# A list scheduler in the kernel in place of a hand-made order: gated linear attention followed by a two-layer MLP

## The chip, the cores and the metric

The kernel runs on one core of a Trainium2 chip. The metric is the device time of one execution in microseconds (us); lower is better. A profiled execution also gives a *span*, from its first to its last instruction.

Ratios are the mean time of one kernel's fast runs over the mean of the other's fast runs of the same rounds, so not quite the ratio of the medians that are quoted beside them. "Fast" leaves out runs that are over 1.5% above the fastest of the same kernel. On both the kernel before spread widely (213.6 to 218.1 us, at granted clocks from 0.984 down to 0.960), so differences between variants are read from their own times and traces, beside a control run of the changed kernel on the first of the two; the changed kernel was not run on the second.

## The reference, cut to what matters

```python
def _attn_ref(q, k, v, alpha):                 # B, H, S, D = 4, 8, 768, 48
    state = np.zeros((B, H, D, D))
    for t in range(S):
        state = alpha[:, :, t, :, None] * state + einsum('bhd,bhe->bhde', k[:, :, t], v[:, :, t])
        y[:, :, t] = einsum('bhd,bhde->bhe', q[:, :, t], state)
    return y

def _moe_ref(x, w_in, w_out):                  # x: 3072 x 384, d_ff = 2048
    return gelu_tanh(x @ w_in) @ w_out         # x: y, the heads side by side
```

The kernel cuts time into six chunks of 128. A chunk of one batch is a unit, two batches of one chunk are a *pair* (twelve pairs), and two pairs are a group.

## The kernel before

For a pair, ScalarE (ACT) takes the logarithm of alpha, PE sums it up over time (`cum`), and ACT takes three exponentials; these are the "decays". VectorE (DVE) multiplies q and k with them. For each unit PE transposes the products, DVE evicts them, PE makes the scores, DVE masks them, PE makes kv and y, and DVE carries the state to the next chunk. y goes through ACT (`x`), is transposed and becomes `xT`, the input of layer 1. Layer 1 needs a gelu on ACT for each of 16 tiles, layer 2 a copy and a store for each result.

The order of all this is written by hand. Ahead of the logarithms the kernel loads the table set that holds ln and exp; the set of the gelu it leaves to the compiler.

```python
LN_EXP_SET = 6
    # ... inside run():
        def decays(p):
            return [lambda: (self.act_set(LN_EXP_SET), self.e_ln(p)),
                    lambda: (self.e_cum(p), self.e_exp(p))]
        # ... the third to sixth pair, for instance:
        run(*decays(p3))
        lc = self.layer1(xT1, gT1, 0, 2)
        _merge(lc, scores(p3), 0.3, 0.9)
        run(*state(p3, xT1, 2)[:2], decays(p4)[0])
        l2 = self.layer2(G[1], gT1, False, 0, 2)
        run(*l2[:1], *state(p3, xT1, 2)[2:], *l2[1:3], decays(p4)[1], *l2[3:])
        # ... groups 3 to 5: layer 1 for a whole group (512 columns), x transposed by DMA
```

The PSUM tiles of layer 1 and layer 2 share one ring of four buffers:

```python
            h = hs[nt] = self.ps.tile([C, (hi - lo) * C], F32, tag="ff", bufs=4, name="hT")
            # ...
            acc[mt] = self.ps.tile([C, self.d_model], F32, tag="ff", bufs=4, name="acc")
```

Of the kernel before, what the change touches and what calls it, by code (L numbers as in the profile page):

```python
# [11 lines left out]
LN_EXP_SET = 6  # L12
DMA_QK = False
# [9 lines left out]
def _merge(main, side, first=0.0, last=1.0):  # L23

    n, m = len(main), len(side)
    lo, hi = first * n, last * n
    at = [lo + (hi - lo) * (i + 0.5) / m for i in range(m)] if m else []
    j = 0
    for i in range(n):
        while j < m and at[j] <= i:  # L30
            side[j]()
            j += 1
        main[i]()
    while j < m:
        side[j]()
        j += 1


class _Kernel:
    def __init__(self, ctx, tc, q, k, v, alpha, w_in, w_out, out):  # L40
# [10 lines left out]
        self.groups = [[(c, b) for b in range(B)] for c in range(self.NCH)]  # L51

        const = ctx.enter_context(tc.tile_pool(name="const", bufs=1))
        self.ld = ctx.enter_context(tc.tile_pool(name="ld", bufs=6))
        self.wk = ctx.enter_context(tc.tile_pool(name="wk", bufs=3))
        self.grp = ctx.enter_context(tc.tile_pool(name="grp", bufs=2))
        self.ps = ctx.enter_context(tc.tile_pool(name="ps", bufs=1, space=bass.MemoryType.PSUM))

        self.ut_h = const.tile([C, C], F16, name="ut_h")
# [4 lines left out]

# [4 lines left out]
        self.NR = 4  # L69
        self.la_ring = [const.tile([C, 2, H, 64], F16, name=f"la{i}") for i in range(self.NR)]  # L70
        self.qp_ring = [const.tile([C, 2, H, 64], BF16, name=f"qp{i}") for i in range(self.NR)]
        self.kp_ring = [const.tile([C, 2, H, 64], BF16, name=f"kp{i}") for i in range(self.NR)]
        self.npair = 0
        self.u = {}
        self.loaded = {}


    def pads(self, ring):
        for t in ring:
            self.nc.vector.memset(t[:, :, :, self.D:64], 0.0)  # L80

    def load(self, n, group, part=None, eng=None):

        C, H, D = self.C, self.H, self.D
        c = group[0][0]
        if (n, c) not in self.loaded:
            self.loaded[n, c] = self.ld.tile([C, len(group), H, D], BF16 if n == "v" else F32, tag=n,
                                             bufs=3, name=n)
        t = self.loaded[n, c]
        lo, hi = (0, len(group)) if part is None else (2 * part, 2 * part + 2)  # L90
        src = self.src[n][lo:hi].rearrange("b h s d -> s (b h) d")[c * C:(c + 1) * C]
        (eng or self.nc.gpsimd).dma_start(t[:, lo:hi].rearrange("t b h d -> t (b h) d"), src)  # L92
        for i in range(lo, hi):
            u = self.u.setdefault(group[i], {})
            u[n] = t[:, i]
            if i % 2 == 0:
                u[n + "pair"] = t[:, i:i + 2]

    def load_w_in(self, part):
        w = self.d_ff // 4  # L100
        sl = slice(part * w, (part + 1) * w)
        self.nc.gpsimd.dma_start(
            self.w_in[:, :, sl], self.w_in_dram.rearrange("(j c) n -> c j n", c=self.C)[:, :, sl])

    def load_w_out(self, part):
        w = self.NFT // 4
        sl = slice(part * w, (part + 1) * w)
        self.nc.gpsimd.dma_start(
            self.w_out[:, sl, :], self.w_out_dram.rearrange("(n c) p -> c n p", c=self.C)[:, sl, :])
# [6 lines left out]


    def e_ln(self, pair):
        u0 = self.u[pair[0]]
        r = u0["ring"] = self.npair % self.NR  # L120
        self.npair += 1
        self.nc.scalar.activation(self.la_ring[r][:, :, :, 0:self.D], u0["apair"], AF.Ln)  # L122

    def e_cum(self, pair):
        nc, D, H = self.nc, self.D, self.H
        u0 = self.u[pair[0]]
        la = self.la_ring[u0["ring"]]
        cum = u0["cum"] = self.ps.tile([self.C, 2, 512], F32, tag="ca", name="cum")
        for i in range(2):
            nc.tensor.matmul(cum[:, i, 0:H * D], self.ut_h, la[:, i, :, 0:D], start=True, stop=True)  # L130
            for p in range(H // 2):
                nc.tensor.matmul(cum[:, i, H * D + p:H * D + p + 1],  # L132
                                 la[:, i, 2 * p:2 * p + 2, :].rearrange("t h d -> t (h d)"),
                                 self.ones, start=True, stop=True, skip_group_check=True)

    def e_exp(self, pair):
        nc, D, H = self.nc, self.D, self.H
        u0 = self.u[pair[0]]
        cum, r = u0["cum"], u0["ring"]
        b8 = self.wk.tile([self.C, 2, H * D], BF16, tag="b8", bufs=2, name="b8")  # L140
        binv8 = self.wk.tile([self.C, 2, H * D], BF16, tag="binv8", bufs=2, name="binv8")
        bend = self.grp.tile([self.C, 2, H // 2], F32, tag="bend", bufs=6, name="bend")
        nc.scalar.activation(b8, cum[:, :, 0:H * D], AF.Exp)  # L143
        nc.scalar.activation(binv8, cum[:, :, 0:H * D], AF.Exp, scale=-1.0)
        nc.scalar.activation(bend, cum[:, :, H * D:H * D + H // 2], AF.Exp)
        qp, kp = self.qp_ring[r], self.kp_ring[r]
        nc.vector.tensor_tensor(qp[:, :, :, 0:D], u0["qpair"],  # L147
                                b8.rearrange("t i (h d) -> t i h d", h=H), op=ALU.mult)
        nc.vector.tensor_tensor(kp[:, :, :, 0:D], u0["kpair"],  # L149
                                binv8.rearrange("t i (h d) -> t i h d", h=H), op=ALU.mult)  # L150
        for i, cb in enumerate(pair):
            self.u.setdefault(cb, {}).update(qp=qp[:, i], kp=kp[:, i], bend=bend[:, i])


    def t_qk(self, cb, evict=None):
        nc, H, C = self.nc, self.H, self.C
        u = self.u[cb]
        t = self.grp.tile([C, 2, H // 2, C], BF16, tag="qkT", bufs=6, name="qkT")
        if DMA_QK:
            nc.sync.dma_start_transpose(t[:, 0], u["qp"].rearrange("t h d -> t (h d)"))  # L160
            nc.sync.dma_start_transpose(t[:, 1], u["kp"].rearrange("t h d -> t (h d)"))
        else:
            ps = self.ps.tile([C, 2, H // 2, C], BF16, tag="yk", bufs=2, name="qkT_ps")
            for j, s in enumerate((u["qp"], u["kp"])):
                for p in range(H // 2):
                    nc.tensor.transpose(  # L166
                        ps[:, j, p, :], s[:, 2 * p:2 * p + 2, :].rearrange("t h d -> t (h d)"), self.ident)
            (evict or nc.vector.tensor_copy)(t, ps)  # L168
        u["qT"], u["kT"] = t[:, 0], t[:, 1]

    def attn(self, cb):
        nc, H, C = self.nc, self.H, self.C
        u = self.u[cb]
        qT, kT = u["qT"], u["kT"]
        at = self.ps.tile([C, 2, H // 2, C], F32, tag="ca", name="at")
        for p in range(H // 2):
            for o in range(2):
                sl = slice(64 * o, 64 * o + 64)
                nc.tensor.matmul(at[:, o, p, :], kT[sl, p, :], qT[sl, p, :], start=True, stop=True)  # L179
        atm = u["atm"] = self.grp.tile([C, 2, H // 2, C], BF16, tag="atm", bufs=6, name="atm")  # L180
        for o in range(2):
            nc.vector.tensor_tensor(atm[:, o], at[:, o],  # L182
                                    self.ut[:, None, :].to_broadcast([C, H // 2, C]), op=ALU.mult)

    def kv(self, cb):
        nc, H, C, D = self.nc, self.H, self.C, self.D
        c, b = cb
        if c == self.NCH - 1:
            return
        u = self.u[cb]  # L190
        kv = self.ps.tile([C, H // 2, 2 * D], F32, tag="yk", bufs=2, name="kv")
        for p in range(H // 2):
            nc.tensor.matmul(kv[:, p, :], u["kp"][:, 2 * p:2 * p + 2, :].rearrange("t h d -> t (h d)"),
                             u["v"][:, 2 * p:2 * p + 2, :].rearrange("t h d -> t (h d)"),
                             start=True, stop=True)
        old, new = self.state[b][c % 2], self.state[b][(c + 1) % 2]
        for o in range(2):
            ps, fs = slice(64 * o, 64 * o + 64), slice(D * o, D * o + D)
            acc = kv[ps, :, fs]
            if c > 0:  # L200
                s = self.wk.tile([C, H // 2, D], F32, tag=f"stmp{o}", name="stmp")
                nc.vector.tensor_tensor(s[ps], acc, old[ps, :, fs], op=ALU.add)  # L202
                acc = s[ps]
# [3 lines left out]
    def y(self, cb, xT, i, dma):  # L207
# [14 lines left out]
        if dma:  # L222
            nc.sync.dma_start_transpose(xT[:, :, i, :], x)
# [10 lines left out]
    def layer1(self, xT, gT, lo=0, hi=4):  # L234
        nc, C = self.nc, self.C
        hs = {}
# [227 lines left out]
```

## Time and profile before

| | before |
|---|---|
| median time | 216.96 us (216.65 to 218.38, 4 runs) |
| span of the profiled run (its time: 214.48) | 212.7 us |
| busy: PE, DVE, ACT, POOL | 86%, 53%, 58%, 25% |
| table loads on ACT | 16 |
| PE matmuls: layer 1, layer 2 | 432, 384 |

The page of a profile gives shares of the whole span; the timeline gives single instructions; the view by windows gives the busy time of each engine in a stretch. Two rows of this last view show weak stretches of the kernel before, after its start. The columns are: from and to, length, then busy time and instructions of PE, of PE's weight loads, DVE, ACT and POOL, granted clock of PE, DMA share and GB/s.

```profile
120.00:132.00 12.00, 9.83 (x110) 6.34 (x107) 9.61 (x22) 6.47 (x12) 0.00 (x0) 0.86 0.27 68
...
175.00:188.00 13.00, 11.92 (x112) 7.54 (x110) 3.49 (x6) 2.14 (x5) 0.00 (x0) 1.00 0.28 77
```

In the first PE is busy for 9.8 of 12 us and runs at a clock of 0.86; its two longest waits there are 1.60 us for a state update by DVE and 0.57 for `x` from ACT. In the second the idle 1.1 us stand at the end, where layer 1 waits for a DMA transpose of `x`. In both the DMA moves 68 to 77 GB/s, beside some 200 earlier, and PE waits for no input.

From 56.6 us on, the waits of PE that the trace of the kernel before names are short and of many kinds: for gelus 2.9 us in all, state updates 2.6, `x` 2.3, a DMA transpose 1.2, a logarithm 0.8, an eviction 0.5.

### The profile page before, as it was taken

The numbers are of one execution on the slowest core, as the hardware profiler recorded it, in microseconds if no ns is written. First come the engines' busy times: TensorE is split into PE (matmuls) and PEld (weight loads), VectorE is DVE, ScalarE is ACT, GpSimd is POOL, SyncE is SP. The second block draws the span as 40 slices with busy tenths as digits, with TensorE's granted clock in tenths as the row PEclk, the third lists the DMA queues.
The fourth block names the chain that finished last, engine by engine and source line by source line (L and its number), as shares of the span: only waits on it lengthen the run. The fifth ranks groups of instructions, "written<-read, shape, count | busy, mean of one in ns | idle before, by whom it ended". The sixth has DMA issues, their size and how long they took to land.

```text
span 212.7 us, 4196 instructions
## 1 busy us (share of the span) xinstructions
PE 183.7 (86%) x1734; PEld 118.1 (56%) x1740; DVE 111.9 (53%) x224; ACT 124.0 (58%) x235; POOL 53.9 (25%) x51
## 2 busy tenths in 40 slices
PE   7676579997688998998868959999989999979993
PEld 2344468664466586576556645545655546634561
DVE  7372470059658558548578796464895652210121
ACT  3327968641785866586894746758638661149400
POOL 7983753656342344345300000000000000000000
PEclk9999999999799999999999997999999999999999
DMA  7999999999999999999993121100222001310022
GB/s 139 168 222 172 204 207 212 173 171 189 208 248 206 186 183 209 187 192 205 189 168 22 44 70 40 37 3 0 74 77 74 0 3 56 112 57 0 0 74 74
DMA packets 42738, 25.82 MB, mean 121 GB/s; under 512 B 32704, under 2 KB 39360, under 8 KB 42720
## 3 DMA queue, kind: packets, MB, share of 16 engines
q0 software_dynamic: 32208, 19.27, 65.4%
q1 hardware_dynamic: 10512, 6.29, 10.9%
q8 instruction: 13, 0.21, 0.5%
q14 instruction: 5, 0.04, 0.1%
HBM read 25.17 MB, written 4.72 MB: 141 GB/s over the span
## 4 chain that ended last, share of the span: by engine, by line
PE 50%; DMA 20%; POOL 8%; issue 8%; DVE 6%; ACT 6%; SPq 0%; POOLq 0%; ACTq 0%; DVEq 0%
PE acc L270 20%; PE hT L241 19%; DMA w_out<-in_moe_w_out_dram 7%; DMA a<-in_alpha_dram 7%; DMA q<-in_q_dram 5%; PE at L179 3%; PE qkT_ps L166 2%; POOL v L92 2%; DVE atm L182 2%; PE cum L130 2%; POOL q L92 2%; POOL a L92 2%; POOL k L92 2%; DVE qkT L168 2%; DMA xT<-x 1%
## 5 line engine op out<-in xcount | busy, mean ns | idle before, releaser
L241 PE MATMUL hT<-xT,w_in 128*128 128x256 bf16 (+1 forms) x427 | 71.7, 311 | 8.0 <-ACT gT L246 5.6
L246 ACT ACTIVATE gT<-hT 128x256 bf16<-128x256 f32 (+1 forms) x144 | 60.7, 457 | 24.1 <-PE hT L241 22.5
L270 PE MATMUL acc<-w_out,gT 128*128 128x384 bf16 x384 | 68.8, 329 | 0.0
L241 PEld LDWEIGHTS <-w_in 128*128 128x128 bf16 x432 | 40.4, 99 | 27.4 <-issue 9.2
L270 PEld LDWEIGHTS <-gT 128*128 128x128 bf16 x384 | 35.7, 98 | 21.9 <-issue 0.8
L182 DVE TENSOR_TENSOR atm<-at,ut 128x512 bf16<-128x512 f32 x48 | 30.9, 686 | 15.2 <-PE at L179 15.1
L274 DVE COPY ot<-acc 128x384 f32<-128x384 f32 x24 | 13.2, 556 | 33.2 <-PE acc L270 32.8
L221 ACT CAST x<-yps 128x384 bf16<-128x384 f32 x24 | 11.5, 478 | 29.0 <-PE yps L218 26.6
L147 DVE TENSOR_TENSOR qp<-q,b 128x768 bf16<-128x768 f32 x12 | 11.5, 958 | 27.3 <-ACT b L143 27.1
L168 DVE COPY qkT<-qkT_ps 128x1024 bf16<-128x1024 bf16 x21 | 14.5, 691 | 15.1 <-PE qkT_ps L166 15.1
L92 POOL DMA_DIRECT2D v<-in_v_dram x9 | 12.0, 1335 | 16.4 <-issue 9.5
L143 ACT ACTIVATE b<-cum 128x768 bf16<-128x768 f32 x12 | 9.7, 810 | 9.7 <-PE cum L132 9.1
L92 POOL DMA_DIRECT2D q<-in_q_dram x9 | 12.1, 1344 | 11.2 <-issue 7.2
L92 POOL DMA_DIRECT2D k<-in_k_dram x9 | 12.0, 1331 | 7.9 <-DVE stmp L202 3.9
L92 POOL DMA_DIRECT2D a<-in_alpha_dram x8 | 10.8, 1353 | 11.7 <-issue 6.8
L179 PE MATMUL at<-qkT 64*128 64x128 bf16 x192 | 9.5, 218 | 4.7 <-DVE atm L182 3.7
L179 PEld LDWEIGHTS <-qkT 64*128 64x128 bf16 x192 | 5.5, 94 | 11.9 <-DVE qkT L168 6.4
L113 ACT ACT_TABLE_LOAD x9 | 11.5, 1283 | 0.9 <-PEq L448 0.7
L149 DVE TENSOR_TENSOR kp<-k,binv 128x768 bf16<-128x768 f32 x12 | 11.4, 952 | 1.2 <-DMA k<-in_k_dram 1.2
L204 DVE TENSOR_TENSOR st<-stmp,bend 64x192 bf16<-64x192 f32 x32 | 11.3, 353 | 1.4
L122 ACT ACTIVATE la<-a 128x768 f16<-128x768 f32 x12 | 10.0, 842 | 2.9 <-DMA a<-in_alpha_dram 2.8
L202 DVE TENSOR_TENSOR stmp<-kv,st 64x192 f32<-64x192 f32 x32 | 11.3, 353 | 0.5
(41 smaller groups left out, 154.6 us busy)
## 6 DMA issues: line engine op xcount, KB each, us to landing
out_dram<-ot SPq DMA_DIRECT2D x24, 192.0 KB, 2.0
q<-in_q_dram POOLq DMA_DIRECT2D x6, 384.0 KB, 13.1
k<-in_k_dram POOLq DMA_DIRECT2D x6, 384.0 KB, 13.3
a<-in_alpha_dram POOLq DMA_DIRECT2D x3, 768.0 KB, 11.8
q<-in_q_dram POOLq DMA_DIRECT2D x3, 768.0 KB, 11.7
k<-in_k_dram POOLq DMA_DIRECT2D x3, 768.0 KB, 12.4
a<-in_alpha_dram POOLq DMA_DIRECT2D x5, 384.0 KB, 13.1
w_in<-in_moe_w_in_dram POOLq DMA_DIRECT2D x4, 384.0 KB, 9.6
```

What stands on the lines that cost most here:

```text
L92: (eng or self.nc.gpsimd).dma_start(t[:, lo:hi].rearrange("t b h d -> t (b h) d"), src)
L113: nc.scalar.add_instruction(mybir.InstLoadActFuncSet(name=nc.get_next_instruction_name(), act_func_set_id=i, engine=mybir.EngineType.Activ ...
L147: nc.vector.tensor_tensor(qp[:, :, :, 0:D], u0["qpair"], b8.rearrange("t i (h d) -> t i h d", h=H), op=ALU.mult)
L149: nc.vector.tensor_tensor(kp[:, :, :, 0:D], u0["kpair"], binv8.rearrange("t i (h d) -> t i h d", h=H), op=ALU.mult)
L168: (evict or nc.vector.tensor_copy)(t, ps)
L179: nc.tensor.matmul(at[:, o, p, :], kT[sl, p, :], qT[sl, p, :], start=True, stop=True)
L182: nc.vector.tensor_tensor(atm[:, o], at[:, o], self.ut[:, None, :].to_broadcast([C, H // 2, C]), op=ALU.mult)
L221: nc.scalar.copy(x, yps.rearrange("t h d -> t (h d)"))
L241: nc.tensor.matmul(h, self.w_in[:, j, nt * C:(nt + 1) * C], xT[:, j, lo:hi].rearrange("p g t -> p (g t)"), start=j == 0, stop=j == self.NK ...
L246: nc.scalar.activation(gT[:, nt, lo * C:hi * C], hs.pop(nt), AF.Gelu_apprx_tanh)
L270: nc.tensor.matmul(acc[mt], gT[:, nt, mt * C:(mt + 1) * C], self.w_out[:, nt, :], start=nt == 0, stop=nt == self.NFT - 1)
L274: nc.vector.tensor_copy(ot, acc[mt])
```

## The change

The hand-made order is replaced by a list scheduler that runs while the kernel is built. Each task has one engine (or a choice of ACT and DVE), a cost, a priority, its dependences and the buffers that it takes. The recurrence has the highest priority. Layer 1 and layer 2 of all pairs are one stream that keeps its order: layer 1 of pair m, layer 2 of pair m. From the third pair on, the decays of pair m+2 have a fixed slot between the gelus of pair m and those of pair m+1, so that the table sets don't alternate. For the first two pairs, k products and evictions are cut in halves. All x transposes are on PE. The diff, cut to its core:

```diff
-LN_EXP_SET = 6
-DMA_QK = False
+LN_EXP, GELU = 6, 0
+W = dict(
+    ln=760, exp=720, bend=170, gelu4=510, gelu2=340, table=1290,
+    cum=530, t8=450, t4=225, attn=340, kv=170, inter=170, intra=205, tx=168, l1_4=655, l1_2=340, l2=655,
+    # ...
+)
+class Scheduler:
+    # ... of the tasks that can start within 60 ns of the earliest, the one of highest priority:
+                    window = min(f[0] for f in found) + 60
+                    at, t = min((f for f in found if f[0] <= window), key=lambda f: (f[1].prio, f[0]))
+    # ... tasks():
+            early = m < 2
+                    e1 = s.add("ev", {"ACT": W["ev4_act"], "DVE": W["ev4"]}, o, self.turned(u, j, "q"), [t1])
+                g = s.add("gelu", {"ACT": W["gelu2"]}, 10000 + n, self.gelu(f, c, lo, hi, nt),
+                          [t] + free + between[m - 1], GELU)
+                ot = s.add("ot", {"DVE": W["ot"], "ACT": W["ot_act"]}, -1, self.result(f, c, b), [t])
+        for m, ps in decays.items():
+            for p in ps:
+                if m >= 0:
+                    lns[p].deps.append(gs[m][-1])
+    # ... run():
+        for t in order:
+            if t.load is not None:
+                self.act_set(t.load)
+            t.emit(t.engine)
```

## The prediction

> **What bounds the kernel now.** I read the page first (busy shares, slices, chain), then the timelines of PE, ACT and DVE for the first 72 us, those of PE and ACT around 105 us, and the POOL timeline.
>
> ```profile
> PE 183.7 (86%) x1734; PEld 118.1 (56%) x1740; DVE 111.9 (53%) x224; ACT 124.0 (58%) x235; POOL 53.9 (25%) x51
> ...
> PE   7676579997688998998868959999989999979993
> ...
> PE 50%; DMA 20%; POOL 8%; issue 8%; DVE 6%; ACT 6%; SPq 0%; POOLq 0%; ACTq 0%; DVEq 0%
> ```
>
> PE is the busiest engine and half of the chain that ended last. But 86% flatters it: it counts warm-up matmuls on a zero tile and the overlapping tails of pipelined matmuls. So I take the spacing of starts from PE's timeline (start, duration, what):
>
> ```profile
> 32.23 5.40 PE L241 MATMUL hT<-xT,w_in 128*128 128x256 bf16 x48 [0.45 <-DVE xT L231]
> 37.47 4.06 PE L270 MATMUL acc<-w_out,gT 128*128 128x384 bf16 x24
> 41.37 0.33 PE L130 MATMUL cum<-la,ut_h 128*128 128x384 f16 x1
> ```
>
> From 32.23 to 37.47 is 5.24 us for the 16 layer-1 tiles of a pair (three matmuls each, 0.3275 a tile). From 37.47 to 41.37 is 24 layer-2 matmuls, 0.1625 each, so 5.20 for a pair's 32. The same timeline gives, per pair: cum 0.53, transposes of q and k 0.89, scores 0.66, kv 0.35, y 0.75, transposes of x 0.33. Sum **13.95 us per pair**; twelve pairs, less the last kv and the first inter-chunk y, are some 166 us of useful PE work in a span of 212.7. About 46 us are waits, warm-ups and cold clock. Where they begin:
>
> ```profile
> 4.85 0.84 ACT L122 ACTIVATE la<-a 128x768 f16<-128x768 f32 x1 [2.83 <-DMA a<-in_alpha_dram]
> ...
> 9.49 0.96 DVE L149 TENSOR_TENSOR kp<-k,binv 128x768 bf16<-128x768 f32 x1 [1.20 <-DMA k<-in_k_dram]
> ...
> 18.04 0.81 PE L241 MATMUL hT<-xT,w_in 128*128 128x256 bf16 x6 [0.45 <-DVE xT L231]
> ```
>
> Layer 1 starts at 18.0: the first k lands at 9.5 and a serial chain follows, in which PE does only 3.2 us of work. Later, layer 1 repeatedly waits for a gelu that stands behind the next decays and a table load on ACT:
>
> ```profile
> 107.28 0.39 PE L166 MATMUL qkT_ps<-ident,kp 128*128 128x128 bf16 x4
> 109.35 0.82 PE L241 MATMUL hT<-xT,w_in 128*128 128x256 bf16 x6 [1.68 <-ACT gT L246]
> ...
> 107.62 1.28 ACT L246 ACT_TABLE_LOAD   x1
> 108.91 1.67 ACT L246 ACTIVATE gT<-hT 128x256 bf16<-128x256 f32 x5
> ```
>
> The first gelu starts at 108.91 and PE's fifth tile, which needs its PSUM buffer, at 109.35, 0.44 later. I use this pattern below.
>
> **What the Trainium skill says.** "ScalarE: Activation LUTs", What ACT_TABLE_LOAD costs: about 1283 ns for the load plus 1380 ns of drain at each switch. The trace agrees on the load (1283 ns mean, 16 loads) and not on the drain: from 107.62 to the gelu at 108.91 is 1.29. Same page, Table sets: gelu and the tanh approximation of gelu are in separate sets, and a compiler pass puts a load before each activation that needs one. In the trace seven loads carry the gelu's own line, so that pass is at work. "TensorE: Matmul & The Clock Gate", Back-to-back issue gap: 262 cycles for 256 columns, so 109 ns; the 48 above took 109 each, so halving layer 1's tiles costs PE almost nothing. "Perfetto Trace Analysis", Identifying the Most-Contended Engine: matmul busy share is no measure of closeness to the roofline; the 184 busy against 166 of work agrees.
>
> **The change, part by part.** The built order of the changed kernel shows it, engine by engine.
>
> *Work.* Layer 1 goes from 432 to 576 matmuls, all 256 wide; groups 3 to 5 ran 512 wide at 0.215, so this adds 0.6 us. The 12 DMA transposes of x become 36 more PE transposes (2.0 us) and 12 DVE copies. Wide gelus (0.56 apart) become pairs at 0.33 apart: some 5 us on ACT. Warm-up matmuls go from 32 to 39. Loads are the same bytes, all by pair, first ones in the same order.
>
> *A mistake in it.* The scheduler charges one table load per change of set, and the kernel emits it as set 0. The built program puts a second load, of set 11, under the gelu's own line straight after: ten loads of set 0 that no activation uses. ACT has 30 loads in place of 16. Each wasted one is 1.28 us of ACT, 12.8 in all. Does it reach PE?
>
> *Steady period*, pairs 3 to 10, counting from T, the end on PE of the second chunk's y. PE then does x transposes, 28 layer-2 matmuls and cum: 0.165 + 0.65 + 0.165 + 1.95 + 0.53 + 1.95 = 5.41 to the end of layer 2. It goes on with four layer-1 tiles (1.31), transposes (0.89), first scores (0.33) and kv (0.18): 2.7 us, then needs a PSUM buffer that the first new gelu frees. ACT's order between gelus is: load, ln, two exps, bend, copy of the *second* layer-2 result, load, load, gelu. The exps end at T + 0.21 (PE to ACT) + 0.42 (x) + 1.28 + 0.84 + 0.84 (cum and its latency) + 1.55 = T + 5.14. The copy must wait for layer 2's end, T + 5.41 + 0.21 = 5.62, takes 0.45, and two loads end at T + 8.64. Tile 5 starts at T + 9.07. PE got there at T + 8.1, so it **waits 0.95 each period**. With one load the gelu would come 0.3 before it is needed. After tile 5: twelve tiles 3.93, kv 0.18, scores 0.33, two y 0.75, four layer-2 matmuls 0.65, in sum 5.84. Period 5.41 + 3.66 + 5.84 = **14.9** against 13.95 of work. DVE needs about 10 to 11 us a period, ACT 13: neither is the bound alone; it is the loop of both through that copy.
>
> *Start.* Halved k products and halved evictions shorten the chain from k's landing (9.5): products 10.0 and 10.5, evictions on ACT to 11.6, scores, masks, y, x; layer 1 near 16.8, 1.2 earlier. The second pair's inputs do not come earlier. POOL's waits tell their landings:
>
> ```profile
> 16.71 0.74 POOL L108 DMA_DIRECT2D w_out<-in_moe_w_out_dram  x1 [1.35 <-DMA a<-in_alpha_dram]
> 18.82 0.74 POOL L108 DMA_DIRECT2D w_out<-in_moe_w_out_dram  x1 [1.37 <-DMA q<-in_q_dram]
> 20.92 1.17 POOL L92 DMA_DIRECT2D a<-in_alpha_dram  x1 [1.36 <-DMA k<-in_k_dram]
> ```
>
> The new order has ACT do ln (16.7), exps (to 19.9), three evictions, the last waiting for k (to 23), and only then two loads: first gelu near 25.6, where it was 23.0. This takes back the early start. From tile 5 at 26.0, 28 tiles and the rest of the recurrence take 10.3, so both layer-1 halves end at 36.3 (was 37.5). Then two layer-2 pairs (10.4), two cums, and the recurrence of pair 2 with the transposes of pair 3, 16.6 us of PE work with fills, and about 1.3 of waits on x and kp: layer 1 of pair 2 at **54.0**. The old kernel is there at 56.6.
>
> *Sum.* From 54.0: first T at 61.0, the next at 76.4 (its layer 2 falls wholly in the period), then seven periods of 14.9: T of period 10 at 180.7, less 0.2 for missing kv. Then 4.88 of layer 2, 5.24 and 5.20 for the last pair: 195.8. The old kernel's last matmul ended at 209.0 with 3.6 more to the span's end, which I keep: span 199.4. The median time is 1.02 times the span (217.05 to 212.7), so 203.5; I say **204**, as a walk with fixed durations misses small waits.
>
> **The rivals.**
> *The second load is hidden.* If the copy does not wait, or the period has slack that I missed, PE is the bound at 13.95: 7.6 us less, about 196. For it: the order was made from durations near the trace's. Against: with the load counted, 3.76 us on ACT stand against 2.7 on PE.
> *The fixed order slips.* One wrong duration repeats in every period; margins of 0.1 to 0.4 for kp before the transposes and for state updates before y are thin. 0.5 more per period and 1 at the start: about 209.
> *Loads bind.* The DMA row is at 9 for half the span. But POOL's spacing is near 2.1 us a strip and 1.5 for v, 7.9 us a pair, against 14.9 of use, and loads run four pairs ahead. They bind only in the first 50 us, where I counted them; if the start gains nothing at all, 206.5.
> *Cold clock.* Granted clock drops to 0.83 and 0.86 in two stretches of before (50 to 60, 120 to 132), beside PE gaps near 2 us. Steady gaps of 1 us should end that. If it came each period, the gain would be gone; I see no reason for it.
>
> **Range and chances.** 196 to 198 if the load is hidden, 209 if orders slip; I put the range at 197 to 209. Faster by 2% means below 212.7, nearly 9 us from my figure, more than any rival but the cold clock gives: 0.95. Within 2%: 0.04. Slower: 0.01.
>
> **What would show it.** 30 table loads, ten under the explicit line with nothing between them and the next load. In a period of 14.9, one PE wait for a gelu near 1 us at layer 1's fifth tile, eight times, and ACT's copy of the result waiting about 0.5 for PE. First gelu near 25.6, layer 1 of pair 2 near 54. No clock drop after 20 us. I would be wrong if the period is 14.0 with no gelu wait, if PE waits mostly on DVE or DMA, or if the start is not earlier at all.

## The result

The changed kernel takes **205.31 us** (median of 4 runs, 204.72 to 206.03) beside 216.96 for the kernel before: ratio 0.9453, 95% interval 0.9394 to 0.9511. It is faster by some 5.5%. On the chip of the experiments the same kernel took 205.01 us, with a ratio of 0.9546 to a kernel before that was somewhat faster there (median 214.76).

The page after: busy shares, the slices of PE and of its granted clock, and the chain that ended last, by engine.

```profile
PE 185.2 (91%) x1925; PEld 133.7 (65%) x1927; DVE 105.6 (52%) x219; ACT 151.0 (74%) x317; POOL 61.3 (30%) x63
...
PE   7786489999899989989989989989989989989992
...
PEclk9999958999999999999999999999999999999998
...
PE 70%; ACT 16%; DMA 6%; POOL 4%; issue 1%; DVE 1%; POOLq 0%; DVEq 0%
```

PE now shows a regular pattern, two full slices and one a little less. ACT went from 6% to 16% of the chain. The clock falls early, in the slices from about 25 to 36 us, and after that it stays up but for the last slice.

One steady period, first in PE's timeline, then in ACT's:

```profile
103.05 0.34 PE L307 MATMUL kv<-v,kp 128*128 128x96 bf16 x4
104.06 0.49 PE L363 MATMUL hT<-xT,w_in 128*128 128x256 bf16 x3 [0.67 <-ACT gT L369]
...
119.11 0.49 PE L363 MATMUL hT<-xT,w_in 128*128 128x256 bf16 x3 [0.66 <-ACT gT L369]
```

```profile
99.97 0.18 ACT L245 ACTIVATE bend<-cum 128x8 f32<-128x8 f32 x1
100.54 0.48 ACT L384 COPY ot<-acc 128x384 f32<-128x384 f32 x1 [0.39 <-PE acc L377]
101.04 1.28 ACT L181 ACT_TABLE_LOAD   x1
102.33 1.28 ACT L369 ACT_TABLE_LOAD   x1
103.62 2.50 ACT L369 ACTIVATE gT<-hT 128x256 bf16<-128x256 f32 x8
```

The fifth layer-1 tile starts at 104.06 and the next period's at 119.11: 15.05 us. ACT waits 0.39 for PE ahead of its copy, makes the copy, loads a set that nothing uses, loads the right one, and starts the first gelu at 103.62; PE follows 0.44 later. PE's four kv matmuls, 0.043 apart, give up its input side at 103.22, so the real gap is 0.84; the 0.67 of the profile counts from the modelled end of the last of them.

The start is another matter. First PE's timeline, then the view by windows:

```profile
26.34 0.80 PE L363 MATMUL hT<-xT,w_in 128*128 128x256 bf16 x3 [2.13 <-ACT gT L369]
...
28.58 3.38 PE L363 MATMUL hT<-xT,w_in 128*128 128x256 bf16 x15
...
57.14 0.82 PE L363 MATMUL hT<-xT,w_in 128*128 128x256 bf16 x6
```

```profile
22.00:33.00 11.00, 8.30 (x82) 5.80 (x83) 5.74 (x13) 7.77 (x16) 7.33 (x7) 0.69 1.28 213
```

The fifteen matmuls from 28.58 need 3.17 us to the next start, 0.211 each, twice the 0.109 of the full clock. The clock records of the trace put the slow stretch at 25.03 to 31.85. So the clock fell in the middle of the wait of 2.13 us that ends at 26.34, after 3.4 us in which PE had been busy for 1.64; two more rows of the view:

```profile
21.61:25.03 3.42, 1.64 (x24) 1.09 (x25) 2.68 (x6) 2.60 (x4) 2.58 (x3) 1.00 1.26 204
25.03:28.44 3.41, 2.10 (x19) 1.24 (x19) 1.40 (x5) 2.46 (x6) 2.05 (x3) 0.50 1.31 203
```

Layer 1 of the third pair (the prediction counts pairs from 0 and calls it pair 2) starts at 57.14, no earlier than in the kernel before (56.56).

So the whole gain lies after that point: from there to the last matmul the old kernel took 152.3 us (56.56 to 208.9) and the new one 143.1 (57.14 to 200.2). By the matmul spacings of the prediction the useful work there is about 133 and 134 us (an estimate), so waits and slow clock together went from some 19 us to 9, and eight gaps of some 0.84 are most of the 9.

### The profile page after: what moved, and what is told of

It reads as the page before. It is cut to its first block, busy times and chain, and to the rows that moved or that the text cites. A ratio compares the mean times of both kernels' runs of the same rounds, so it can differ in the third digit from the quotient of the medians.

```text
span 204.1 us, 4664 instructions
## 1 busy us (share of the span) xinstructions
PE 185.2 (91%) x1925; PEld 133.7 (65%) x1927; DVE 105.6 (52%) x219; ACT 151.0 (74%) x317; POOL 61.3 (30%) x63
## 4 chain that ended last, share of the span: by engine, by line
PE 70%; ACT 16%; DMA 6%; POOL 4%; issue 1%; DVE 1%; POOLq 0%; DVEq 0%
PE acc L377 31%; PE hT L363 27%; DMA k<-in_k_dram 6%; ACT L369 6%; ACT L181 6%; PE at L290 2%; PE yps L339 2%; ACT ot L384 2%; ACT gT L369 2%; PE cum L232 2%; PE yps L336 2%; PE xT_ps L353 2%; POOL q L202 1%; PE qkT_ps L268 1%; PE kv L307 1%
## 5 line engine op out<-in xcount | busy, mean ns | idle before, releaser
L363 PE MATMUL hT<-xT,w_in 128*128 128x256 bf16 x576 | 74.9, 278 | 8.1 <-ACT gT L369 7.9
L369 ACT ACTIVATE gT<-hT 128x256 bf16<-128x256 f32 x192 | 62.0, 388 | 6.1 <-PE hT L363 5.6
L363 PEld LDWEIGHTS <-w_in 128*128 128x128 bf16 x576 | 54.6, 99 | 17.5 <-issue 9.4
L181 ACT ACT_TABLE_LOAD x20 | 25.7, 1283 | 1.1 <-PEq L576 0.7
L384 ACT COPY ot<-acc 128x384 f32<-128x384 f32 x18 | 8.6, 478 | 16.9 <-PE acc L377 16.7
L202 POOL DMA_DIRECT2D a<-in_alpha_dram x11 | 12.7, 1153 | 20.7 <-ACT la L222 13.4
L278 DVE COPY qkT<-qkT_ps 128x1024 bf16<-128x1024 bf16 (+1 forms) x21 | 13.3, 673 | 7.6 <-PE qkT_ps L268 7.6
L357 DVE COPY xT<-xT_ps 128x384 bf16<-128x384 bf16 x24 | 8.5, 356 | 16.6 <-PE xT_ps L353 16.5
L202 POOL DMA_DIRECT2D q<-in_q_dram x12 | 14.0, 1163 | 9.9 <-DVE qp L257 4.2
L369 ACT ACT_TABLE_LOAD x10 | 12.8, 1283 | 0.1
L257 DVE TENSOR_TENSOR kp<-k,binv 128x768 bf16<-128x768 f32 (+1 forms) x14 | 11.6, 837 | 2.4 <-DMA k<-in_k_dram 2.4
L190 PE MATMUL idle<-zero 128*128 128x512 bf16 x37 | 11.3, 432 | 1.3 <-DVE zero L542 1.2
```

The source lines that it names most:

```text
L181: nc.scalar.add_instruction(mybir.InstLoadActFuncSet(name=nc.get_next_instruction_name(), act_func_set_id=i, engine=mybir.EngineType.Activ ...
L190: self.nc.tensor.matmul(ps, self.zero[:, 0:self.C], self.zero, start=True, stop=True)
L202: (nc.sync if e == "SP" else nc.gpsimd).dma_start(t.rearrange("t b h d -> t (b h) d"), src)
L257: self.nc.vector.tensor_tensor(u[n + "p"][:, lo:hi, :, 0:self.D], u[n][:, lo:hi], u["b" if n == "q" else "binv"][:, lo:hi], op=ALU.mult)
L278: self.copy(e)(t, u.pop(("T_ps", i, which)))
L363: self.nc.tensor.matmul(h, self.w_in[:, j, nt * self.C:(nt + 1) * self.C], self.xT[c][:, j, lo:hi].rearrange("p g t -> p (g t)"), start=j ...
```

## The experiments

The theory: in the steady part PE and ACT form a loop through ACT's copy of the second layer-2 result and the *two* table loads, and the wasted load makes it longer than PE's work. The rivals: PE's work or DVE set the period and the second load hides; only the number of table loads counts; the DMA transposes were the old kernel's loss; the order matters little.

### e1_one_load: no wasted load

```diff
-LN_EXP, GELU = 6, 0
+LN_EXP, GELU = 6, 11
```

> The set that the scheduler loads for the gelus is 11 in place of 0, so the ten wasted loads go (20 loads in place of 30); the order of everything else is the same. My theory (loop of PE and ACT through the copy of the second layer-2 result): in the changed kernel PE's fifth layer-1 tile starts 0.84 us after PE was free for it in each steady period of 15.05; with the gelus 1.28 earlier the wait goes and the period becomes about 14.2, over eight periods 6.7 us less. At the start the first gelu comes at 24.6 in place of 25.9, and the stretch at a granted clock of 0.69 from 22 to 33 us shrinks by an unknown amount: 1.3 to 4 us less. Sum: 194.5 to 197.5 us. Rival (PE's own work and its waits on DVE set the period, the second load hides in ACT's slack): no steady change, at most the 1.3 us at the start, 203.5 to 205.

Measured: **196.99 us** (196.48 to 197.41), correct. There are 20 loads. ACT's and PE's timelines of a period:

```profile
97.64 1.28 ACT L181 ACT_TABLE_LOAD   x1
98.93 1.21 ACT L369 ACTIVATE gT<-hT 128x256 bf16<-128x256 f32 x4
```

```profile
99.65 0.34 PE L307 MATMUL kv<-v,kp 128*128 128x96 bf16 x4
99.83 0.49 PE L363 MATMUL hT<-xT,w_in 128*128 128x256 bf16 x3
```

The fifth tile follows kv without a wait, and the period is 14.23 (the same row of fifteen layer-1 matmuls starts at 88.87 and at 103.10). The steady part became 0.82 a period shorter, as the theory says: less than the 1.28 of the load, as PE's own work (13.95 by the prediction) is now nearly the whole period. The third pair's layer 1 starts at 55.29, 1.85 earlier. Eight periods and the start would be 8.4 us; 8.0 were measured against the control. The load did reach PE, and the rival that it hides is out.

### e2_three_loads: one more useless load

```diff
             if t.load is not None:
                 self.act_set(t.load)
+                if t.load == GELU:
+                    self.act_set(LN_EXP)
```

> A further needless load (of set 6) between the two that stand before the first gelu of each pair: 40 loads, all else the same. My theory: ACT is on the loop, so each period gets the whole 1.28 us, 16.3 in place of 15.05; eight periods 10.3 us and 1.3 or more at the start: 216.5 to 219 us. Rival (the loads have slack): under 4 us more, below 209.5.

Measured: 223.43 us (222.85 to 223.97), 18.4 over the control and more than the theory's 219. PE's timeline:

```profile
109.83 0.49 PE L363 MATMUL hT<-xT,w_in 128*128 128x256 bf16 x3 [1.95 <-ACT gT L369]
...
126.18 0.67 PE L363 MATMUL hT<-xT,w_in 128*128 128x256 bf16 x3 [1.95 <-ACT gT L369]
126.64 0.53 PE L307 MATMUL kv<-v,kp 128*128 128x96 bf16 x4
126.97 2.12 PE L363 MATMUL hT<-xT,w_in 128*128 128x256 bf16 x9
```

The wait is 1.95, which is 0.66 and the whole 1.28. The period is 16.34 where the clock stays up (16.3 expected): the dose adds in full. In the next period the same wait is followed by nine matmuls in 2.05 us, at half speed; that period takes 17.91, with a mean clock of 0.90. The view by windows shows how the two differ:

```profile
105.87:109.28 3.41, 2.00 (x32) 1.50 (x31) 2.74 (x5) 3.40 (x3) 1.68 (x2) 1.00 0.91 215
...
122.93:126.35 3.42, 1.45 (x23) 0.94 (x20) 3.30 (x7) 3.40 (x6) 0.98 (x1) 1.00 0.95 214
126.35:129.76 3.41, 3.41 (x26) 2.19 (x25) 0.47 (x3) 2.07 (x7) 0.00 (x0) 0.50 0.35 68
```

The clock changes only at instants that lie a multiple of 3.41 us apart. The wait ahead of 126.18 fell wholly between two of them, which left PE busy for 1.45 of the 3.4 us, and the clock went down; the wait ahead of 109.83 was cut in two by one, at 109.28, and the clock stayed. The trace has four such slow stretches after the start. The part above the expectation is about what they cost (an estimate: four times 17.91 less 16.34 is 6.3 us), and I had not counted it.

### e3_copy_between: the copy after the first load

```diff
+        act = [t for t in order if t.engine == "ACT"]
+        for a, t in zip(act, act[1:]):
+            if t.load == GELU and a.kind == "ot":
+                a.load, t.load = GELU, None
```

> Both loads stay, but ACT's copy of the second layer-2 result stands after the set-0 load, not ahead of both, in the steady slots (30 loads; the first two gelu phases are unchanged). My theory: the 0.39 us that ACT waits for PE ahead of the copy is inside the loop; with the load done in that time the gelus come some 0.4 earlier, period 14.65 in place of 15.05, in all 3 us less: 201.5 to 203 us. Rival (the loop does not run through this copy; the two loads after the exps alone matter, or DVE sets the period): no change, 204.5 to 206.

Measured: **202.44 us** (201.40 to 202.56), correct. ACT's timeline:

```profile
98.85 1.28 ACT L181 ACT_TABLE_LOAD   x1
100.15 0.48 ACT L384 COPY ot<-acc 128x384 f32<-128x384 f32 x1
100.65 1.28 ACT L369 ACT_TABLE_LOAD   x1
101.94 2.50 ACT L369 ACTIVATE gT<-hT 128x256 bf16<-128x256 f32 x8
```

The useless load now fills the time in which ACT waited for PE, the copy waits for nothing, and the period is 14.69 (rows at 90.96 and 105.65; 14.65 expected). With the number of loads unchanged this gains 2.6 us: the loop does run through the wait of this copy.

### e4_halves_once: halves for the first pair only

```diff
-            early = m < 2
+            early = m < 1
```

> The halved k products and halved evictions are used for the first pair only, not for the second; both loads stay. The second pair's evictions go to DVE, so ACT can load tables right after its exps. My theory of the start: first gelu at 22.7 in place of 25.9, fifth layer-1 tile at 23.1 in place of 26.3, PE's gap of 2.1 us before it gone and with it most of the slow clock from 25 to 33 us; layer 1 of the second pair ends near 36 in place of 39.2. Time 201 to 203.5 us, steady period unchanged at 15.05. Rival (the second pair's late k, at 21 us, sets the start whatever ACT does): within 1 us of the changed kernel, 204.5 to 206.

Measured: 204.53 us (204.19 to 204.90), only 0.5 under the control. PE's timeline:

```profile
23.03 0.70 PE L363 MATMUL hT<-xT,w_in 128*128 128x256 bf16 x3 [3.65 <-ACT gT L369]
...
32.72 5.41 PE L363 MATMUL hT<-xT,w_in 128*128 128x256 bf16 x48 [0.24 <-DVE xT L357]
```

The first gelu came at 22.60, as I expected, and the fifth tile at 23.03. But the scheduler put the transposes of the second pair behind this tile, so PE stood still for 3.65 us and the clock fell here too (0.84 from 22 to 33 us). The second pair's layer 1 then waits for its own `xT` at 32.72 and ends at 37.97, where I had said 36 (39.22 in the changed kernel). My theory of the start falls in this form: an earlier first gelu alone does not make the start shorter.

### e5_both and e7_warm_start: the start once more

e5 has the edits of e1 and e4. e7 adds ten matmuls on a zero tile in PE's gap:

```diff
+            if (c, lo, nt) == (0, 0, 4):
+                ps = self.tile("yk", [self.C, 512], F32, "idle")
+                for _ in range(10):
+                    self.nc.tensor.matmul(ps, self.zero[:, 0:self.C], self.zero, start=True, stop=True)
```

The scheduler has warm-up tasks of its own, but they take a buffer of the ring `ff`, and in this gap all four of its buffers wait for the gelus. So the edit uses the other ring.

> One load (set 11) and the halved products and evictions for the first pair only. The two earlier runs told 197.0 (one load) and 204.5 (halves once, both loads). If the start is set by the second pair's chain and the slow clock, not by ACT's first gelu, the early gelu (near 21.3 us) brings little: 195.5 to 197.5 us. If the first gelu sets it, 1.28 and 3.3 us earlier add up: 193 to 195 us. Period 14.23 in both cases.

> The same as the run with both edits, plus ten matmuls on the zero tile in PE's gap ahead of the fifth layer-1 tile (19.4 to 21.7 us), written to a free buffer of the other PSUM ring. My theory of the missing start: after a gap near 2 us the granted clock falls to about half for several us just where the second pair's chain and layer 1 run, and this costs about 2.5 us. With the gap filled the clock stays at 1.0 from 22 to 33 us, the second pair's layer 1 ends near 35 in place of 37 to 38, and the time is 2 to 3 us under the run with both edits, about 193 to 194.5 us. Rival (the late k and the serial chain alone set it): no difference over 0.7 us, whatever the clock does.

Measured: e5 **196.40 us** (195.15 to 196.75), e7 **195.17 us** (194.90 to 195.45), both correct. The view by windows, e5 and then e7:

```profile
22.00:33.00 11.00, 9.96 (x106) 7.77 (x108) 6.89 (x14) 5.17 (x17) 7.40 (x7) 0.84 1.29 216
```

```profile
22.00:33.00 11.00, 10.53 (x129) 8.49 (x128) 6.52 (x14) 7.32 (x24) 7.54 (x7) 1.00 1.29 214
```

With the zero matmuls the clock stays at 1.0. The third pair's layer 1 starts at 52.98 in e7 and 54.79 in e5, 1.8 us apart; the medians differ by 1.2. The one e5 run whose mean clock was 1.0 took 195.15 us, as e7 does. The clock is a real part of the start's loss, but smaller than the 2 to 3 us that I expected. The median of e5 is 0.6 below that of e1, but their runs overlap (195.15 to 196.75 and 196.48 to 197.41). e7 is the best version: ratio 0.9096 to the kernel before, interval 0.9038 to 0.9153.

### e6_no_slots: decays without fixed slots

```diff
-                          [t] + free + between[m - 1], GELU)
+                          [t] + free, GELU)
 ...
-                    lns[p].deps.append(gs[m][-1])
+                    pass
```

> The fixed slots for the decays are undone (no dependence of a pair's logarithm on the last gelu, none of gelus on the decays); both loads as in the changed kernel. The order that comes out has 15 table loads in place of 30, as two pairs' decays share a gap. If table loads on ACT are what costs, 15 fewer should bring at least as much as the ten wasted ones: below 198 us. My theory (only the length of one gap counts): a gap with two pairs' decays is some 2.4 us of exps and ln longer and its PE wait grows by about that, the gap left out saves one wait of 0.84; two periods take about 30.1 plus 1 to 2 us. Sum over five double gaps: 205 to 213 us, with waits of PE for gelus of 2 to 3.5 us in every second period and a slow clock after some of them.

Measured: 213.30 us in the one fast run, 216.7 to 218.3 in three that are slow. The built order has 15 table loads, half of the changed kernel's. Still its fast run is 8 us above the control. PE's timeline of the profiled run, which was a slow one:

```profile
84.69 2.06 PE L363 MATMUL hT<-xT,w_in 128*128 128x256 bf16 x9 [2.31 <-ACT gT L369]
```

Two pairs' decays stand in one gap, PE waits 2.31 for the gelu, and the nine matmuls after it take 2 us, at half speed. This wait must not be read as a size in the fast state. But the fast run is enough against the rival, which wanted less than 198 us, and it is just above the 205 to 213 of my own theory: fewer table loads do not make the kernel faster if the gap between two sets of gelus gets longer. How much of its 8 us is the wait and how much the clock (0.965 in this run, 0.983 in the control) stays open.

### b1_pe_transposes: the old order with PE transposes

In the kernel before, the last three groups get `self.t_x(...)` in place of the DMA transpose:

```diff
-                side += [lambda i=i: self.yk(G[g][i], xT, i) for i in range(4)]
+                for i in range(4):
+                    side += [lambda i=i: self.yk(G[g][i], xT, i, False)]
+                    side += [lambda i=i: self.t_x(G[g][i - 1], xT, i - 1)] if i else []
+                side += [lambda: self.t_x(G[g][3], xT, 3)]
```

(The same is done for groups 3 and 4, between the decays.)

> The kernel before with one part of the change alone: the last three groups transpose x on PE and DVE, not by DMA; its hand-made order is kept. If the DMA transposes were the main loss of the old kernel's second half (layer 1 of the last group starts 1.2 us after PE is free and about 3 us after the last y's copy), this takes at least half of the 9.4 us that the change gains there: 208 to 211 us. My theory (the old waits are spread over gelus, scores and state updates at many places, and only a whole new order removes them): 3 us of wait go, 2.0 us of PE work come, so 213 to 217 us, beside 213.6 to 218 for the kernel before on this chip.

Measured: fast runs 217.86 to 219.42 us, beside 213.60 to 216.20 for the fast runs of the kernel before in this batch: ratio 1.0173, 95% interval 1.0070 to 1.0276. By the limit of 2% the verdict is unclear, but the interval leaves out 1, and the times lie above even what my own theory said. This part of the change, put alone into the old order at these places, brings no gain. So the gain does not come from the removal of the DMA transposes by itself; the new order with DMA transposes was not run. Its profiled run was a slow one, so where its loss lies stays open. It was run on another chip.

### e8_layers_first: the same scheduler, priorities turned round

```diff
-            u, P = self.p[c, i], 100 * m
+            u, P = self.p[c, i], 100 * m + 50000
```

> The changed kernel with the priority of the recurrence put below that of the layers, the scheduler and all tasks else the same. The order that comes out runs each pair's 48 layer-1 and 32 layer-2 matmuls as one block and the recurrence after it. My theory: recurrence first is what gives the interleaving; without it the chain from transposes over evictions, scores, masks and y to the next layer 1 (some 8 us, of which PE works 3.5) stands bare in every period, so a period is 18 to 19 us and the time 235 to 250 us, with PE waiting mostly on DVE. Rival (the order matters little as PE is bound by its own work and ACT's loop): under 212 us.

Measured, on the chip of b1: 269.99 us (269.47 to 271.82), worse than I expected. PE's timeline:

```profile
130.06 7.48 PE L363 MATMUL hT<-xT,w_in 128*128 128x256 bf16 x48
137.38 5.36 PE L377 MATMUL acc<-w_out,gT 128*128 128x384 bf16 x32
...
151.34 7.11 PE L363 MATMUL hT<-xT,w_in 128*128 128x256 bf16 x48
```

Layer 1 and layer 2 stand as blocks. From the end of layer 2 (142.57) to the next layer 1 (151.34) the recurrence takes 8.8 us, as expected. But the period is 21.3, not 18 to 19: layer 1 alone takes 7.3 in place of 5.24, as the clock is down when it starts (mean clock of this run 0.848). With the tasks, costs and number of table loads the same, the priority alone is worth some 65 us, across the two chips, on which the kernel before took about the same.

The other parts of the change (layers by pair in place of by group, narrower gelus) were not tried alone.

### The control

> The changed kernel itself, unaltered, as the control on this chip, since the kernel before took 213.6 to 217.9 us in the first batch and 216.7 to 218.4 in the first measurement. I expect 203.5 to 206 us, 30 table loads, a steady period of 15.05 us with a wait near 0.66 us in the profile (0.84 from the last matmul's slot) for the first gelu.

Measured: 205.01 us (204.51 to 205.43) with a wait of 0.66 in each period, as before.

## Why the prediction was right or wrong

The time was right (204 predicted, 205.3 measured, within the range of 197 to 209), and so was the mechanism of the steady part. But two steps were wrong, and that they cancelled was luck.

- **The steady period.** Predicted 14.9 with a PE wait of 0.95 for the gelu at the fifth tile; measured 15.05 with a gap of 0.84, and a further 0.17 where the first scores wait for an eviction by DVE. The loop named was the right one: e1, e2 and e3 changed its links one at a time, and the period went to 14.23, 16.34 and 14.69, within 0.05 of what was written before each run.
- **The wasted load.** Right in kind and number, and its cost was found: that of the steady ones in e1's period, that of the early ones only within e1's total. Of the twenty loads under the explicit line, ten were useless. The rival "the second load is hidden" is refuted by e1 and by e2.
- **"Layer 1 of pair 2 at 54.0."** Wrong: 57.14. The first steps held (layer 1 at 16.68, first gelu at 25.91, fifth tile at 26.34 against 16.8, 25.6 and 26.0). The step that failed is "28 tiles and the rest of the recurrence take 10.3": they took 12.9, at a granted clock of 0.69 from 22 to 33 us. So layer 1 of the third pair was not earlier than before, which is near one of the prediction's own signs of being wrong, a start "not earlier at all". I had written "no clock drop after 20 us", on the ground that steady gaps of 1 us are too short, and had not looked at how little PE has to do ahead of the fifth tile: in the trace it waits for 0.89, 1.25 and 2.13 us between 19.4 and 26.3. The last of them alone is not it: the clock fell in its middle, and in e1, where this wait is 0.33, the clock fell as well (22.14 to 28.97). e7 shows that filling PE's gap keeps the clock up, worth 1.2 to 1.8 us in the order of e5. For the changed order itself no such run was made. An estimate: PE was busy for 5.5 us at half speed there, of which up to half, 2.8 us, can be the clock's; whether that is the whole loss of 2.6 stays open.
- **"The median time is 1.02 times the span."** Wrong. The profiled run of the kernel before was a fast execution, 214.48 us beside a median of 217; time and span of one execution differ by 1.8 us only. From my span of 199.4 the time should have been 201.2. The measured span was 204.1: 3.1 of the difference came from the start, about 1.05 from seven periods of 0.15 more, the rest from small pieces at the first period and the tail. The factor of 1.02 added 2.3 us too many, and rounding up to 204 added 0.5.
- **"Loads bind" and "the fixed order slips".** The steady periods agree to a few hundredths, and PE waits for no load in them: in the trace after, it waits for gelus and, briefly, for DVE.
- **"Cold clock."** I gave this rival little, as the steady gap is short. That was right for the steady part and wrong for the start; e2 and e8 show that it is near: in both it adds to the other loss.

Two small slips: layer 1's narrower tiles add some 0.4 us by the spacings that the prediction gives (288 times 0.109 less 144 times 0.215), not 0.6, and DVE is busy for 9.5 us in a period, not 10 to 11. Neither changes the sum.

On the skill: "TensorE: Matmul & The Clock Gate", What's actually happening, says that the clock has two states and falls to half after an idle window of about 3.4 us, and that these windows run on whatever the kernel does. The spacing of 0.211 in place of 0.109 agrees with the two states. So does the window: in the twelve traces the slow stretches between 10 us and the last matmul last 3.41, 6.83 or 10.24 us, and begin in the middle of a gap (25.03 in the changed kernel) or well after one (22.71 in e5, where the gap ended at 21.24). But the window need not be idle. By the view by windows the clock fell after each one in which PE was busy for less than 41%, after none above 56%, and after some between.

## What to carry to other kernels

Draw the loop through all engines for one steady period, with what each in-order queue puts between two links: here a copy that waits for PE stood ahead of two table loads, and moving a link or adding one gave its length, and dropping one gave 0.82 of its 1.28 us, until PE's own work was the bound. Look at the built order, not only at the scheduler's costs; the cost table knew one load where two were emitted. And when a span is turned into a time, compare the profiled run's own time with its span, not with the median of other runs.

## What the Trainium skill lacked or had wrong

- "ScalarE: Activation LUTs" gives 1380 ns of drain on top of each load of 1283 ns. Here a load is followed by the gelu after 1.29 us (107.62 to 108.91 before, 102.33 to 103.62 after), and two loads in a row start 1.29 apart; no drain is seen.
- The same page says that a compiler pass puts a load before an activation that needs one. It does not say that a set loaded by hand that lacks the function costs a whole second load in silence: 30 loads in place of 20 here, and 8.0 us from 205.0 to 197.0.
- "TensorE: Matmul & The Clock Gate" advises against PE gaps over about 3 us. The slow state came with shorter ones: in e1 at 22.14, where PE had been busy for 1.21 of the last 3.41 us and no wait was over 1.65, and in e2 with waits of 1.95. Gaps of 0.84, one in 15 us, never brought it.
- No page gives the difference between the device time and the span from first to last instruction; here it was 1.7 to 1.9 us in each run. ("Runtime: NRT & Kernel Launch", The ~15µs preamble/postamble breakdown, gives about 6.2 us between a profile's total time and the runtime's time, which is another pair.)
